# Attention into a maxout FFN on one core: a new hand-written order for batches 0 and 1, and new counts of FFN units per gap

## The chip, the core and the metric

One core of a Trainium2 chip. The time is device microseconds (us) of one execution; three runs of the kernel before gave 296.02, 296.65 and 298.34, median 296.65. The engines are TensorE (PE; its weight loads are PEld), VectorE (DVE), ScalarE (ACT), GpSimd (POOL) and SyncE (SP), which only issues DMA transfers. GpSimd issues some transfers as well, those that turn float32 into bfloat16 on the way.

## What is computed

```python
scores = scale * np.matmul(q, k_all.transpose(0, 1, 3, 2))   # 8 batches, 8 heads, 576 queries, 16+576 keys, D 64
scores = np.where(causal, -1000000000.0, scores)             # the 16 beacon keys are never masked
a = np.exp(scores - scores.max(-1, keepdims=True))
a /= a.sum(-1, keepdims=True) + 1e-09
x = np.matmul(a, v_all)                                      # regrouped to 4608 tokens x 512
h = np.maximum(np.maximum(x @ w1, x @ w2), x @ w3)           # 512 x 768 each
out = h @ w_out                                              # 768 x 512
```

## The kernel before, in words

Heads are taken in pairs: 4 pairs to a batch, 32 in all; two pairs make a quad (0 to 15), and quads 2b and 2b+1 are batch b. For a pair, q and k are brought into transposed form (qT, kT, four buffers each). Pairs 0 to 15 are transposed on TensorE ("half" and "whole" steps, L438, L387, and L396 later), pairs 16 to 31 by DMA: cast to bfloat16, stored to DRAM and fetched with a transposing transfer (`store_pair`, `fetch_pair`, L370, L377). Beacon keys are copied into kT apart ("keys", L458).

The scores of a pair come in four groups (pair, group), each a few matmuls into one PSUM tile (L512), followed by one exponential on ScalarE (L527) that writes `at_sb`. Where a group holds the diagonal it is masked in place: either by GpSimd with an affine select (L546) or by VectorE, which multiplies with a triangle (L544). The values of a quad are taken in two halves of the queries, (quad, 0) and (quad, 1): `emit_pv` (L587) first sums with a column of ones, then multiplies with v; ScalarE inverts the sums (logarithm L607, exponential L609), VectorE multiplies into `xT` (L619), where the tokens of four batches have room.

The FFN is cut into 198 units, 22 for each of 9 blocks of 512 tokens: 18 of x times a weight (L649; the first block in halves, L668), each ending in a copy or a maximum into `hT` on VectorE (L657, L659, L676, L678), and 4 of `hT` times w_out (L685) that are copied to y (L697) and stored. A unit may run as soon as its tokens are in xT; it needs a PSUM bank.

PSUM: a ring of score tiles (two `sc`, and from `widen` on a third, `wide`), two `pv` banks, and at first two `ffn` banks. Scores, transposes, second halves of values and pairs of FFN units ("double") take ring tiles in turn; first halves and single units take the pv banks. Who wants a bank waits for its last reader.

The order of every engine's work is the order in which the program is written (a manual schedule): each engine takes its own instructions strictly in turn. There are two parts.

- Batches 0 and 1 are a list, `first_steps`, run from top to bottom. A step names what is issued, for instance `("mask", 5, 0, "dve")`. `busy n` and the last number of `scores` are spare matmuls on constant data (L476) that keep TensorE occupied, `idle n` such matmuls with half the rows (L417), and the last two numbers of `half` idle transposes ahead of k and of q. `ffn bank kind` is one FFN unit. Loads in the list go to SP, or to GpSimd's own queue (`load w`, `load quad`, `load quad half`, `load w_out`). A gate is a one-element memset by VectorE or GpSimd into the target of a load (L198, L286): the load then waits until that engine has come so far.
- From quad 4 on a loop runs, in which a quad issues: three groups of scores of its first pair, both halves of the values of the quad before, masks, inversion and products; then bursts of further scores with "gaps" between them, each filled with FFN units. `gaps[quad]` has six numbers: the first two stand between the values and the first burst (three groups of scores), the third behind it, the fourth ahead of the second burst (two groups), the last two behind it. A unit whose tokens aren't ready is left out, and so is a double whose two units don't belong together. If the count of units done is odd, one is put ahead of the quad. What is left runs alone at the end.

Casts of the float32 loads run on GpSimd (pairs L248, v L301, first v tiles L313), some on ScalarE. Staging buffers (`st`, eight of them) bound how far SP loads ahead.

## Time and profile before

| | |
|---|---|
| median of three runs | 296.65 us |
| the profiled execution | 297.69 us |
| its span, first to last instruction | 295.80 us |
| mean granted TensorE clock | 0.998 |
| TensorE busy | 281.4 us (95%) |
| VectorE, ScalarE, GpSimd busy | 176.9, 147.5, 116.0 us |
| moved by DMA | 49.51 MB, 167 GB/s over the span |
| TensorE reaches the scores of pair 8 (quad 4) | 60.9 us |

A line of the chain gives start, length and what it was; the chain runs back from the last instruction to what released it each time. A line of a timeline gives start, length, engine, line of the kernel, operation, output<-inputs and count; in brackets is the idle time ahead of it and what ended it. Busy shares of TensorE hold spare matmuls too.

### The profile page before, as it was taken

Reading aid. Unit: us, or ns where it says so; the run is one execution under the profiler, and the core shown is the slowest. Engines: PE = TensorE matmul, PEld = TensorE weight load, DVE = VectorE, ACT = ScalarE, POOL = GpSimd, SP = SyncE. Lnnn points to the kernel's source line nnn. Section 1 sums busy time; section 2 is a strip of 40 time slices with the busy share of each in tenths; the row PEclk is TensorE's granted clock in tenths of the full one; section 3 lists DMA queues with packets and bytes.
Section 4 is the critical chain, followed back from the end, with each engine's and each line's share of the span. In section 5 each row is a group of like instructions: output and inputs, shape, how many; then the busy total and the mean of one; then the engine's idle time right before and its main releaser. Section 6 shows DMA issues by size and latency. Waiting matters only on the chain.

```text
span 295.8 us, 8837 instructions
## 1 busy us (share of the span) xinstructions
PE 281.4 (95%) x3673; PEld 159.1 (54%) x3699; DVE 176.9 (60%) x321; ACT 147.5 (50%) x232; POOL 116.0 (39%) x236
## 2 busy tenths in 40 slices
PE   6899897899999999999999999999999999999995
PEld 3556675664644545454546777545454545444442
DVE  1764678866576566546664656465746564474273
ACT  2665475863834687566735573545555551300300
POOL 3647227253644584436444572357425220000000
PEclk9999999999999999999999999999999999999999
DMA  6999999999986898879898999999658002101103
GB/s 129 157 180 192 201 224 231 192 203 241 248 225 179 201 264 217 190 173 248 224 221 136 232 209 216 211 161 216 189 123 224 2 0 109 38 0 71 71 3 143
DMA packets 95096, 49.51 MB, mean 167 GB/s; under 512 B 64976, under 2 KB 89808, under 8 KB 95056
## 3 DMA queue, kind: packets, MB, share of 16 engines
q1 hardware_dynamic: 89408, 43.73, 63.1%
q0 software_dynamic: 5648, 5.21, 11.5%
q8 instruction: 29, 0.48, 0.8%
q14 instruction: 11, 0.09, 0.1%
HBM read 35.13 MB, written 14.22 MB: 167 GB/s over the span
## 4 chain that ended last, share of the span: by engine, by line
PE 82%; DMA 5%; DVE 5%; ACT 4%; issue 2%; POOL 1%; SPq 0%; ACTq 0%; POOLq 0%
PE pv L649 22%; PE sc L649 12%; PE wide L649 8%; PE sc L685 6%; PE pv L685 6%; PE sc L512 6%; PE sc L587 4%; PE pv L587 4%; DMA whole<-in_k_dram 4%; PE wide L685 3%; PE wide L587 3%; PE wide L512 2%; DVE at_sb L544 2%; ACT at_sb L527 2%; DMA bk<-in_beacon_k_dram 1%
## 5 line engine op out<-in xcount | busy, mean ns | idle before, releaser
L527 ACT ACTIVATE at_sb<-sc 128x736 bf16<-128x736 f32 (+5 forms) x93 | 77.7, 864 | 57.1 <-PE sc L512 56.9
L649 PEld LDWEIGHTS <-w_sb 128*128 128x128 bf16 x648 | 60.7, 98 | 60.6 <-issue 6.1
L546 POOL TENSOR_SCALAR_AFFINE_SELECT at_sb<-at_sb 128x256 bf16<-128x256 bf16 (+3 forms) x138 | 50.4, 383 | 106.4 <-ACT at_sb L527 105.5
L649 PE MATMUL pv<-xT,w_sb 128*128 128x512 bf16 (+1 forms) x337 | 70.8, 349 | 0.4
L527 ACT ACTIVATE at_sb<-wide 128x736 bf16<-128x736 f32 (+3 forms) x35 | 29.9, 855 | 26.0 <-PE wide L512 26.0
L659 DVE TENSOR_TENSOR hT<-hT,pv 128x512 bf16<-128x512 bf16 x50 | 33.8, 685 | 12.9 <-PE pv L649 12.8
L649 PE MATMUL sc<-xT,w_sb 128*128 128x512 bf16 (+1 forms) x183 | 40.4, 361 | 0.6 <-issue 0.2
L248 POOL CAST p<-st 96x768 bf16<-96x768 f32 x40 | 31.9, 821 | 10.7 <-DMA q_dram<-p 10.6
L685 PEld LDWEIGHTS <-hT 128*128 128x128 bf16 x210 | 19.9, 98 | 23.6 <-DVE hT L659 1.0
L619 DVE TENSOR_TENSOR xT<-pv,recip 128x288 bf16<-128x288 f32 (+2 forms) x48 | 14.2, 349 | 28.6 <-ACT recip L609 28.6
L512 PE MATMUL sc<-qT,kT 64*128 64x288 bf16 (+6 forms) x292 | 28.4, 277 | 3.1 <-ACT qT L451 2.5
L512 PEld LDWEIGHTS <-kT 64*128 64x128 bf16 x400 | 14.8, 94 | 25.1 <-issue 17.1
L659 DVE TENSOR_TENSOR hT<-hT,sc 128x1024 bf16<-128x1024 bf16 (+1 forms) x17 | 18.4, 1090 | 13.7 <-PE sc L649 13.7
L587 PEld LDWEIGHTS <-v_sb 128*32 128x32 bf16 (+1 forms) x1408 | 24.6, 96 | 2.3 <-issue 1.0
L649 PE MATMUL wide<-xT,w_sb 128*128 128x512 bf16 (+1 forms) x111 | 24.5, 364 | 0.1
L657 DVE CAST hT<-pv 128x512 bf16<-128x512 f32 x24 | 16.2, 687 | 7.2 <-PE pv L649 7.2
L685 PE MATMUL sc<-w_out_sb,hT 128*128 128x512 bf16 x79 | 19.1, 380 | 0.3
L301 POOL CAST v_sb<-st 128x1536 bf16<-128x1536 f32 (+2 forms) x21 | 18.4, 893 | 2.1 <-issue 2.1
L685 PE MATMUL pv<-w_out_sb,hT 128*128 128x512 bf16 x81 | 18.9, 379 | 0.3 <-issue 0.2
L668 PEld LDWEIGHTS <-w_sb 128*128 128x128 bf16 x144 | 13.3, 98 | 3.9 <-issue 1.4
L609 ACT ACTIVATE recip<-lnd 128x288 f32<-128x288 f32 x32 | 14.2, 443 | 1.0
L697 DVE COPY y<-pv 128x512 f32<-128x512 f32 x14 | 9.7, 691 | 8.1 <-PE pv L685 7.5
(112 smaller groups left out, 286.2 us busy)
## 6 DMA issues: line engine op xcount, KB each, us to landing
st<-in_q_dram SPq DMA_DIRECT2D x48, 144.0 KB, 3.8
st<-in_k_dram SPq DMA_DIRECT2D x48, 144.0 KB, 3.9
st<-in_v_dram SPq DMA_DIRECT2D x24, 256.0 KB, 5.2
out_dram<-y SPq DMA_DIRECT2D x9, 512.0 KB, 3.4
out_dram<-y SPq DMA_DIRECT2D x17, 256.0 KB, 2.8
w_sb<-in_moe_w_dram POOLq DMA_DIRECT2D x6, 384.0 KB, 7.4
q_dram<-p SPq DMA_DIRECT2D x16, 144.0 KB, 2.8
k_dram<-p SPq DMA_DIRECT2D x16, 144.0 KB, 2.4
```

Of the source, the lines that this page charges most:

```text
L248: cast(t16.rearrange("p r h d -> p h r d"), st[0:QP, i * NQ2 : (i + 1) * NQ2].rearrange("p (h r d) -> p h r d", h=2, r=QR),)
L301: cast(v_sb[0:n, t:t1].rearrange("p t h d -> p (t h d)"), st[0:n, (t - t_lo) * H * D : (t1 - t_lo) * H * D],)
L512: nc.tensor.matmul(ps[:, e, off : off + q1 - q0], kT[hs, 128 * t : 128 * t + 128], qT[hs, q0:q1], start=True, stop=True, tile_position=(64 ...
L527: nc.scalar.activation(out=both_heads(p, gi), in_=ps[:, :, 0 : g_width(p, gi)], func=AF.Exp, scale=scale)
L546: nc.gpsimd.affine_select(out=view, in_=view, compare_op=ALU.is_ge, fill=0.0, base=x0, pattern=[[0, 2], [1, hi - lo]], channel_multiplier=-1,)
L587: nc.tensor.matmul(ps[bank][32 * j : 32 * j + 32, lo + q0 - qa : lo + qb - qa], lhsT, at_view(PPQ * quad + j // 2, t, j % 2, q0, qb), star ...
L609: nc.scalar.activation(out=recip, in_=lnd, func=AF.Exp, scale=-1.0)
L619: nc.vector.tensor_mul(xT[:, 2 * g + part - 1, c0 + ca : c0 + cb], ps[bank][:, lo : lo + cb - ca], recip[:, ca:cb],)
L649: nc.tensor.matmul(dst[:, o0 : o0 + n], w_in[i][:, ct, 128 * (ft + f) : 128 * (ft + f + 1)], xT[:, ct, x0 : x0 + n], start=(ct == 0), stop ...
L657: (by_act if alone[0] else by_dve)(h, ps)
L659: nc.vector.tensor_max(h, h, ps)
L685: nc.tensor.matmul(ps[:, t - tt] if two else ps, hT[:, ft, 128 * t : 128 * (t + 1)], w_out_sb[:, ft, :], start=(ft == 0), stop=(ft == n_ft ...
```

## The change

It touches the list and the counts, and the helpers that the list needs. In the list:

- Start: GpSimd makes the triangle first and then issues its two quad loads; SP loads q of pair 1, k and q of pair 0, k of pair 1, then the beacon keys; before it was k of pair 1, q and k of pair 0, keys, q of pair 1. The first v load is gated by GpSimd instead of VectorE. 27 spare matmuls stand ahead of the first transposes (19 before, with 4 `idle` ones, which go), and 42 more idle transposes, in three turns.
- 16 of the 32 masks were on VectorE, 14 are now: (1,0), (1,2), (1,3), (2,2), (3,3), (5,3), (6,1), (6,2), (6,3) go to GpSimd and (1,1), (2,1), (3,1), (3,2), (4,0), (4,1), (5,1) come from it.
- The loads of w2, of the second whole quad of batch 1, of v of batch 1 and of pair 9 come later in the list, those of w_out and the cast of pair 9 earlier; several get gates. Four copies of transposed q and k change between ScalarE and VectorE.
- The list has 17 FFN units as before, in other places.

By quad, 4 to 15, the counts of units that really run are (up to the next quad's start, with the odd ones): before 11, 14, 10, 12, 9, 13, 10, 11, 12, 10, 11, 14; after 12, 12, 13, 10, 8, 16, 12, 10, 14, 8, 6, 14.

```diff
--- before.py
+++ after.py
     def L(fn, *a):
-        return lambda: fn(*a)
+        return lambda *more: fn(*a, *more)
...
-    def load_v(b, piece):
+    def load_v(b, piece, gate=None):
         for t in range(*V_PIECES[piece]):
-            load_v_tile(b, t, v_stage(b, t))
+            dst = v_stage(b, t)
+            if gate and t == V_PIECES[piece][0]:
+                gate.memset(dst[32:33, 0, 0:1], 0.0)
...
-    def next_load(n=1):
+    def next_load(n=1, gate=None):
         for _ in range(n):
             if loads:
-                loads.pop(0)()
+                loads.pop(0)(*([idle[gate]] if gate else []))
...
     first_steps = [
+        ("triangle",),
+        ("load quad half", 1, 0),
+        ("busy", 17),
+        ("load half", 1, 0, "sp"),
+        ("load half", 0, 1, "sp"),
+        ("load half", 0, 0, "sp"),
+        ("identity",),
+        ("cast half", 1, 0, "dve"),
         ("load half", 1, 1, "sp"),
-        ("load half", 0, 0, "sp"),
-        ("load half", 0, 1, "sp"),
         ("load keys 0", "sp"),
-        ("load quad half", 1, 0),
-        ("busy", 15),
+        ("load v0", 0, "pool"),
         ("cast half", 0, 1, "dve"),
-        ("idle", 2),
-        ("load half", 1, 0, "sp"),
-        ("cast half", 1, 1, "dve"),
-        ("triangle",),
-        ("load v0", 0, "dve"),
-        ("busy", 4),
+        ("busy", 10),
         ("cast keys 0", "act"),
-        ("identity",),
         ("cast half", 0, 0, "act"),
-        ("half", 0, 0, "ffn", "act", 0, 0),
+        ("half", 0, 0, "ffn", "act", 0, 7),
+        ("load v0", 1, "pool"),
+        ("cast half", 1, 1, "act"),
         ("turn keys 0",),
+        ("half", 1, 0, "ffn", "dve", 2, 5),
         ("keys", 2, "pool"),
+        ("keys", 3, "act"),
+        ("keys", 1, "act"),
+        ("load quad half", 0, 1),
+        ("scores", 0, 0, 3),
+        ("half", 3, 0, "ffn", "dve", 0, 0),
+        ("load w", 0),
+        ("mask", 0, 0, "dve"),
         ("cast v0", 0),
-        ("scores", 0, 0, 1),
-        ("keys", 3, "act"),
-        ("keys", 1, "dve"),
-        ("load v0", 1),
-        ("cast half", 1, 0, "dve"),
-        ("half", 1, 0, "pv", "dve", 0, 0),
-        ("half", 3, 0, "ffn", "dve", 0),
         ("scores", 1, 0, 4),
-        ("half", 2, 0, "pv", "dve", 6),
-        ("load quad half", 0, 1),
+        ("half", 2, 0, "pv", "dve", 6, 0),
+        ("mask", 1, 0, "pool"),
+        ("cast v0", 1),
+        ("load v0", 2),
         ("scores", 3, 0, 3),
-        ("mask", 1, 0, "dve"),
-        ("scores", 2, 0, 5),
-        ("mask", 0, 0, "dve"),
-        ("load v0", 2),
-        ("cast v0", 1),
+        ("scores", 2, 0, 4),
         ("cast v0", 2),
-        ("load w", 0),
-        ("values", 0, 0, "pv"),
+        ("values", 0, 0, "pv", 0, 4, 0),
+        ("half", 0, 1, "ffn", "act", 0, 7),
+        ("load quad half", 1, 1),
         ("invert",),
+        ("scores", 0, 2, 7),
+        ("mask", 3, 0, "dve"),
         ("mask", 2, 0, "dve"),
-        ("load quad half", 1, 1),
-        ("half", 0, 1, "ffn", "dve", 0, 0),
-        ("mask", 3, 0, "dve"),
-        ("scores", 0, 2, 7),
+        ("scores", 0, 3, 0),
         ("multiply",),
+        ("values", 1, 0, "ffn", 0, 4, 0),
+        ("invert",),
+        ("mask", 0, 3, "pool"),
+        ("half", 1, 1, "pv", "act", 0, 0),
         ("load keys 1",),
-        ("values", 1, 0, "ffn"),
-        ("invert",),
-        ("scores", 0, 3),
-        ("half", 1, 1, "pv", "dve", 0, 0),
-        ("mask", 0, 3, "pool"),
         ("load v0", 3, "dve"),
+        ("multiply",),
+        ("scores", 0, 1, 0),
         ("load v0", 4, "pool"),
-        ("multiply",),
-        ("scores", 0, 1, 2),
-        ("scores", 1, 2, 3),
+        ("scores", 1, 2, 2),
+        ("ffn", "ffn", 0),
         ("ffn", "ffn", 0),
         ("mask", 0, 1, "pool"),
-        ("scores", 1, 3),
-        ("mask", 1, 3, "dve"),
+        ("load w", 1),
+        ("scores", 1, 3, 0),
+        ("half", 2, 1, "pv", "dve", 0, 0),
+        ("scores", 1, 1, 0),
         ("ffn", "ffn", 0),
-        ("load w", 1),
-        ("ffn", "ffn", 0),
-        ("scores", 1, 1, 0),
+        ("cast v0", 3),
+        ("half", 3, 1, "pv", "dve", 0, 0),
         ("load quad", 1, 0),
         ("mask", 0, 2, "pool"),
+        ("scores", 2, 3, 0),
+        ("mask", 1, 1, "dve"),
+        ("mask", 1, 3, "pool"),
+        ("mask", 1, 2, "pool"),
+        ("cast v0", 4),
+        ("load v", 1, 0, "dve"),
+        ("scores", 2, 2, 7),
+        ("cast keys 1", "pool"),
+        ("scores", 3, 2, 3),
+        ("values", 0, 1, "pv", 0, 4, 0),
+        ("scores", 3, 3, 0),
+        ("invert",),
+        ("ffn", "ffn", 0),
+        ("multiply",),
+        ("mask", 2, 3, "pool"),
+        ("turn keys 1",),
         ("load w", 2),
-        ("mask", 1, 1, "pool"),
-        ("cast v0", 3),
-        ("cast v0", 4),
-        ("half", 2, 1, "pv", "dve", 0),
-        ("scores", 2, 2, 6),
-        ("mask", 1, 2, "dve"),
-        ("half", 3, 1, "ffn", "dve", 0),
-        ("load quad", 1, 1),
-        ("mask", 2, 2, "dve"),
-        ("scores", 2, 3, 0),
-        ("scores", 3, 2, 2),
-        ("values", 0, 1, "pv", 0, 4, 0),
-        ("invert",),
         ("scores", 2, 1),
...
+        ("scores", 5, 3, 0),
+        ("load quad", 1, 1),
+        ("mask", 4, 0, "dve"),
+        ("load v", 1, 1, "pool"),
+        ("keys", 7, "pool"),
+        ("mask", 4, 2, "dve"),
         ("mask", 5, 0, "dve"),
-        ("scores", 5, 1),
-        ("mask", 4, 0, "pool"),
-        ("scores", 5, 2),
...
-        ("whole", 6, "ring", "act"),
+        ("whole", 6, "ring", "dve"),
+        ("mask", 5, 2, "dve"),
+        ("mask", 5, 1, "dve"),
+        ("ffn", "ring", 0),
+        ("keys", 6, "act"),
         ("cast v", 1, 0),
-        ("mask", 5, 2, "dve"),
-        ("mask", 5, 1, "pool"),
+        ("ffn", "pv", 1),
+        ("scores", 6, 2, 0),
+        ("scores", 6, 0, 0),
         ("cast pair", 8),
-        ("mask", 4, 3, "pool"),
-        ("ffn", "ring", 0),
-        ("ffn", "pv", 0),
-        ("scores", 6, 2),
+        ("ffn", "pv", 1),
+        ("load w_out",),
+        ("scores", 6, 1, 0),
+        ("values", 2, 0, "ring", 0, 4, 0),
+        ("load", 1, "pool"),
+        ("cast pair", 9),
+        ("invert",),
         ("keys", 9, "pool"),
-        ("scores", 6, 0, 0),
-        ("load", 2),
-        ("scores", 6, 1, 0),
-        ("cast v", 1, 1),
-        ("mask", 5, 3, "dve"),
-        ("ffn", "pv", 0),
-        ("values", 2, 0, "ring", 0, 4, 0),
-        ("invert",),
-        ("keys", 8, "act"),
-        ("mask", 6, 0, "dve"),
-        ("mask", 6, 1, "dve"),
         ("whole", 7, "ring"),
         ("ffn", "pv", 1),
         ("multiply",),
+        ("load", 2, "dve"),
         ("scores", 6, 3, 0),
-        ("mask", 6, 2, "dve"),
+        ("cast v", 1, 1),
+        ("mask", 6, 2, "pool"),
+        ("mask", 6, 1, "pool"),
+        ("mask", 6, 3, "pool"),
         ("scores", 7, 2, 0),
+        ("load", 1, "dve"),
+        ("load", 1, "dve"),
+        ("keys", 8, "pool"),
         ("whole", 8, "pv", "dve"),
         ("scores", 7, 1, 0),
-        ("mask", 6, 3, "dve"),
-        ("load", 1),
-        ("load", 1),
-        ("scores", 7, 0),
-        ("load", 1),
-        ("values", 2, 1, "ring"),
+        ("scores", 7, 0, 0),
+        ("mask", 6, 0, "dve"),
+        ("values", 2, 1, "ring", 0, 4, 0),
         ("invert",),
+        ("scores", 7, 3, 0),
+        ("mask", 7, 2, "pool"),
+        ("whole", 9, "ring", "act"),
         ("multiply",),
-        ("scores", 7, 3, 1),
-        ("load w_out",),
-        ("ffn", "pv", 1),
+        ("mask", 7, 3),
         ("mask", 7, 1, "pool"),
-        ("cast pair", 9),
-        ("mask", 7, 3),
-        ("whole", 9, "ring", "dve"),
+        ("load", 1, "pool"),
+        ("ffn", "pv", 0),
         ("mask", 7, 0, "pool"),
...
     gaps = {
-        4: (2, 2, 2, 1, 1, 2),
-        5: (4, 2, 1, 1, 4, 2),
-        6: (2, 2, 1, 2, 1, 2),
-        7: (2, 2, 1, 7, 1, 1),
-        8: (3, 1, 2, 2, 0, 1),
-        9: (3, 1, 0, 1, 2, 5),
-        10: (5, 0, 1, 2, 0, 2),
-        11: (3, 0, 0, 3, 4, 3),
-        12: (4, 2, 2, 0, 1, 2),
-        13: (2, 2, 3, 6, 1, 1),
-        14: (3, 0, 1, 2, 2, 2),
-        15: (2, 2, 1, 4, 3, 2),
+        4: (3, 2, 2, 2, 1, 1),
+        5: (4, 2, 3, 2, 2, 0),
+        6: (2, 2, 2, 2, 2, 2),
+        7: (1, 1, 1, 7, 1, 1),
+        8: (1, 0, 2, 1, 3, 1),
+        9: (4, 2, 1, 5, 2, 6),
+        10: (5, 0, 2, 2, 1, 2),
+        11: (5, 1, 1, 2, 0, 3),
+        12: (7, 1, 2, 2, 0, 2),
+        13: (3, 1, 3, 14, 2, 3),
+        14: (2, 0, 2, 0, 0, 2),
+        15: (7, 0, 4, 4, 1, 1),
     }
```

## The prediction

> **What bounds the kernel now.** I read the page first (busy shares, slices, chain), then busy time by stage, then the chain of waits and the timelines of the first 62 us, last single quads.
>
> ```profile
> PE 281.4 (95%) x3673; PEld 159.1 (54%) x3699; DVE 176.9 (60%) x321; ACT 147.5 (50%) x232; POOL 116.0 (39%) x236
> DMA  6999999999986898879898999999658002101103
> PE 82%; DMA 5%; DVE 5%; ACT 4%; issue 2%; POOL 1%; SPq 0%; ACTq 0%; POOLq 0%
> ```
> ```profile
> 8.00:34.00 26.00, 24.01 (x437) 15.69 (x431) 17.02 (x49) 16.92 (x28) 15.80 (x31) 1.00 1.12 185
> 34.00:60.00 26.00, 22.39 (x442) 17.20 (x443) 20.82 (x39) 17.05 (x27) 9.18 (x17) 1.00 1.12 213
> 60.00:126.00 66.00, 64.98 (x854) 34.51 (x859) 42.47 (x71) 39.27 (x65) 34.35 (x68) 1.00 0.89 219
> 126.00:189.00 63.00, 62.37 (x938) 38.80 (x946) 36.25 (x62) 35.33 (x55) 30.21 (x61) 1.00 0.92 211
> ```
>
> The second fence has, by stage: its ends and length, busy us (and instructions) of PE, PEld, DVE, ACT, POOL, then the granted clock, the DMA share and GB/s. TensorE carries 82% of the chain. From 60 us on it idles 1 us in 66; from 8 to 60 us it idles 5.6 us, and part of its busy time there is idle work (34 spare matmuls in scores, 19 ahead). So an order can win a few us before 60 and can mostly only lose after. The granted clock is 1.00 from 8 us on: nothing to gain there. The DMA engines run at 9 tenths until 200 us.
>
> ```profile
> 2.25 4.44 DMA bk<-in_beacon_k_dram
> 12.12 1.93 DVE at_sb L544 x6
> 22.96 11.02 DMA whole<-in_k_dram
> 34.02 0.45 PE fps L387 x12
> 43.91 3.64 DVE at_sb L544 x2
> 48.85 0.65 ACT qT L451
> ```
> ```profile
> 29.88 2.64 PE L668 MATMUL fps<-xT,w_sb 128*128 128x256 bf16 x22 [0.34 <-DMA w_sb<-in_moe_w_dram]
> 34.02 0.45 PE L387 MATMUL fps<-ident,whole 96*64 96x96 bf16 x12 [0.80 <-DMA whole<-in_k_dram]
> 49.54 0.58 PE L512 MATMUL sc<-qT,kT 64*128 64x464 bf16 x6 [2.21 <-ACT qT L451]
> ```
>
> The first fence is the chain (start, length, what): six links that are not TensorE's own work. The second shows TensorE's idle time in brackets. The 2.21 us come from the DVE link: two masks on VectorE take 3.64 us (one mask: median 275, longest 2303 ns in the view of at_sb) while GpSimd works without a break:
>
> ```profile
> 43.91 3.64 DVE L544 TENSOR_TENSOR at_sb<-at_sb,tri 128x224 bf16<-128x224 bf16 x2
> 43.73 1.46 POOL L301 CAST v_sb<-st 128x1536 bf16<-128x1536 f32 x1 [2.13 <-issue]
> 45.47 1.59 POOL L248 CAST p<-st 96x768 bf16<-96x768 f32 x2
> ```
>
> Behind them in VectorE's order stand an FFN maximum (0.67), kT of pair 6 (0.74), then ScalarE's qT (0.65), and only then scores (6,2).
>
> **The change, part by part.** The sum is made on the profiled execution: 297.69 us (span 295.80 and 1.89 around it), 1.04 over the median 296.65; I apply it to the median.
>
> 1. *Start, to the first FFN unit (20.3 us).* GpSimd makes the triangle (0.22 + 0.29) before its two quad loads (issue 0.81 + 0.67), so the SP loads meet them later. The beacon keys go from fourth to fifth on SP (0.50 later), and ScalarE casts k of pair 1 (0.51) ahead of the key copies. The first exponential, at 9.31 now, can come 1.3 later (0.50 + 0.51 + copies 0.33) or 0.6 earlier; nearest to the middle, I take 0. The value tiles' gate moves from VectorE (memset at 6.88) to GpSimd behind the identity, near 4.2, so three v loads go 2.7 us earlier. Mask (1,0) on GpSimd costs 0.32 to 0.41 an instruction against 0.28, and two v casts (0.61 each) stand behind it, awaited by values (0,0): I place their end near 14.9 (now 15.1). ScalarE takes q of pair 0 and pair 1 from VectorE, which lets the multiply of quad 1 end 0.6 sooner. First FFN unit: -0.4 (ends -0.9, +1.5).
> 2. *21 to 36 us.* The loads of GpSimd's queue land one behind the other, some 2 us apart: whole k of quad (1,0) landed 11.02 after its issue, at 33.98. In the new order cast v0 3 (waits for its load, 25.4 now, 0.6 earlier by its gate) stands ahead of this load, so it is issued at about 25 instead of 22.3. It still has only the two pieces of w1 ahead; w2 goes behind the keys' cast, and the second whole load behind mask (3,3). By the present spacing it lands at 33.5, with v of batch 1 issued later perhaps at 31. TensorE reaches these transposes at 32.4 (work 1.1 less between). I take -0.8 (ends -1.6, and +4 should the landing keep 13 to 15 us, as whole of quad (1,1) took). w2 and w_out are needed over 6 and 3 us after they land; if that cover is gone each costs its lateness.
> 3. *44 to 54 us.* Mask (5,0) moves ahead of cast v(1,0), and so pays 0.28 twice instead of 3.64. Masks (5,2), (5,1) come behind q and k of pair 6, both now on VectorE (0.75 + 0.75, ScalarE's 0.65 gone), and still meet cast pair 8. Nearest row 2.30 for such a mask, best 0.28: I take 1.8 for the two. Waiting behind them on VectorE: three FFN results, the first in the ring tile that scores (6,1) need, 0.85 late. Of the idle 2.21 this leaves 0.85, and 0.2 goes with qT: -1.2 (ends -2.2, +3.4).
> 4. *54 us to the values of quad 3.* In the present order cast pair 9 (two of 0.82) stands between the masks of pair 7, and the stretch from values (2,1) idles 0.51 + 0.30, then about 1 us before the values of quad 3. In the new order pair 9 is cast before whole 7 and four masks end GpSimd's list. The gate memset of pair 14 on VectorE waits for cast v(1,1), and whole 8's copies stand behind it: 0.4 late. -0.9 (ends -1.6, +1).
> 5. *Idle work.* 8 spare matmuls more (0.135 warm), 42 idle transposes more (half of 0.04 each), 4 idle matmuls gone: 1.7 us of TensorE. All but the seven pairs in turn (0,1), 0.28, lie in waits for the first casts; counted in 1. Uncovered: +1.7.
> 6. *Gaps.* FFN units are only moved, so time is lost only where a gap gets too short. Quads 7 and 8 had 4 units behind the second values, the first two in a free ring tile; now 2 and 1, single, in banks that the multiply still reads (in quad 7 values end at 113.65, the multiply of half 0 at 114.44): +0.7 each. Quad 14 has two instead of three. Quad 11 shows what three small ones cost:
>
> ```profile
> 174.66 0.89 DVE L619 TENSOR_TENSOR xT<-wide,recip 128x288 bf16<-128x288 f32 x3 [0.72 <-ACT recip L609]
> 175.46 1.21 DVE L659 TENSOR_TENSOR hT<-hT,sc 128x1024 bf16<-128x1024 bf16 x1
> 176.73 0.34 PE L512 MATMUL sc<-qT,kT 64*128 64x288 bf16 x4 [0.28 <-DVE hT L659]
> ```
>
>    The double's tile is free 3.5 us after the values' end (173.20), and the third scores need it. With 1.73 of units and 0.4 of scores TensorE waits 1.3: +1.3 for quad 14; quads 11 and 9, now fuller, give back 0.5 and 0.7. Sum +1.5 (ends 0, +3).
>
> *DMA.* Costed at 0: attention of quads 10 to 13 gets later by the units moved ahead. Pair 24's transposes were issued at 178.3 and used at 186.5, landing in 3 to 4.3: some 3 us of cover; gone, up to +2.2.
>
> Sum: -0.4 - 0.8 - 1.2 - 0.9 + 1.5 = -1.8, so 296.65 - 1.8 = 294.85, say 294.8.
>
> *A rule beside this.* In the row one mask stood 2.30 us, across two casts, a mask and a copy of GpSimd. The Trainium skill, "SBUF — State Buffer", section "SBUF: two separate sides", says VectorE with two SBUF inputs and GpSimd take a shared port pair for a whole instruction, the loser waiting fully. The trace agrees that it waits, not that one instruction is its length. By that rule each mask of step 3 waits for one cast (0.82) at most, and it is 0.3 better: 294.5. It speaks against step 1 too: masks put on GpSimd hold the pair 0.1 longer each.
>
> **Rivals.**
> - *All of the early gain stays.* The gaps cost nothing since ScalarE runs ahead of the rows I used, and the masks of step 3 meet no cast: 294.8 - 1.5 - 0.85 = 292.4. For it: TensorE idles only 1 us in 66 past 60. Against: quad 11's wait.
> - *No change.* Early time is given back to the DMA engines (9 tenths): the pairs' loads end when they did, 2 us return: 296.8. For it: the DMA row. Against: 8 us and more of cover until quad 9.
> - *Slower: VectorE stands through GpSimd's whole run.* In the new order cast v(1,0) 1.46, pair 8 1.59, w_out's issue 0.85, pair 9 1.59, v(1,1) 1.21 and three masks 1.2 follow each other, 7.9 us, if pair 9's load has landed. Masks (5,2), (5,1), started 1.8 in, would stand 6.1 instead of 1.8, with TensorE behind them: 294.8 + 4.9 (with its own late copies) = 299.7. It decides from a stand of 6 us on. For it: a mask stood across four instructions. Against: pair 9 is loaded so late that GpSimd should pause before its cast.
>
> **How the numbers follow.** About 1% (3 us) is what a measurement of this kernel can tell from no change. Forecast 0.46 (within 1.5 of 294.8), of which 0.10 lies under 293.7; all of the gain 0.20; no change 0.14; slower 0.20, of which 0.19 is over 299.6. Faster 0.30, same 0.51, slower 0.19. The range takes in the two outer cases but for their far halves: 291.8 to 299.5.
>
> **What would show it.** Right: scores (6,2) without the 2.21, quad 4's first scores 2 to 3 us earlier than 60.9, 0.7 to 1.3 of idle time at the first scores behind the values of quads 7, 8, 14. Wrong: whole of quad (1,0) landing past 33.5, a mask on VectorE over 2.3 us behind 44 us, or DMA named as releaser after 150 us.

## The result, and the profile after

The changed kernel takes 297.52 us (median of 20 runs, 296.75 to 299.72); before, beside it on the same chip, 295.98 (293.92 to 301.15). The ratio is 1.0064, 95% interval 1.0036 to 1.0092: 1.9 us slower, with 1.1 to 2.7 in the interval. (Ratios leave out executions that took over 1.5% more than the fastest of their kernel; medians hold all, and by them the difference is 1.5.) The forecast was 1.8 faster. The profiled executions are 298.05 (span 296.3) and 297.69 (span 295.8), so the profile of before is one of its longer executions, and a comparison of these two shows only 0.5 of the difference.

The page after, then busy time by stage (columns as in the prediction):

```profile
PE 284.5 (96%) x3722; PEld 160.6 (54%) x3745; DVE 169.4 (57%) x310; ACT 149.5 (50%) x236; POOL 118.1 (40%) x247
DMA  8699998999998899799989998996492002101203
PE 85%; ACT 5%; DVE 3%; DMA 2%; issue 2%; POOL 2%; SPq 1%; ACTq 0%; POOLq 0%
```
```profile
8.00:34.00 26.00, 23.34 (x453) 15.22 (x448) 12.56 (x38) 17.82 (x32) 14.64 (x34) 1.00 0.96 156
34.00:60.00 26.00, 25.21 (x475) 19.04 (x475) 19.81 (x48) 18.68 (x30) 12.44 (x28) 1.00 1.05 209
60.00:126.00 66.00, 64.22 (x843) 34.09 (x848) 41.11 (x69) 39.37 (x65) 33.87 (x66) 1.00 0.98 226
126.00:189.00 63.00, 62.17 (x850) 37.62 (x852) 36.37 (x60) 33.35 (x51) 29.36 (x58) 1.00 0.97 222
```

TensorE idles 0.8 us from 34 to 60 where it idled 3.6, but 2.7 instead of 2.0 from 8 to 34, and 1.8 instead of 1.0 from 60 to 126. Part of its busy time before 34 is idle work. The chain of waits at the start is where the time went:

```profile
2.75 6.19 DMA bk<-in_beacon_k_dram
8.96 0.62 ACT bk L867
9.57 0.42 ACT h L220
10.40 0.40 ACT qT L451
10.80 0.41 ACT h L220
11.54 0.20 POOL kT L463
12.01 1.33 POOL quad L229 x2
13.90 0.56 POOL w_sb L326
14.46 0.62 POOL v_sb L316
15.07 0.90 POOL at_sb L551 x3
15.97 1.12 POOL v_sb L316 x2
17.13 0.66 PE pv L592 x24
```

Start, length, what: the beacon keys land at 8.94 us (before: 6.69). ScalarE casts them, then q of pair 0, then k of pair 1 (the step `cast half 1 1`, below also k of pair (1,1)). GpSimd copies the keys, and only then comes to two quad issues, two weight issues, a cast, the mask that was VectorE's, and two casts. Before, the chain went from the keys to the first scores and VectorE's masks. The three places that the forecast named in the middle did improve. The masks on VectorE behind 44 us now take 1.27 for five instructions, and GpSimd's long cast of v begins as the fifth does:

```profile
45.93 1.27 DVE L549 TENSOR_TENSOR at_sb<-at_sb,tri 128x224 bf16<-128x224 bf16 x5
46.93 1.59 POOL L304 CAST v_sb<-st 128x1536 bf16<-128x1536 f32 x1
48.47 1.65 POOL L248 CAST p<-st 96x768 bf16<-96x768 f32 x2
```

The wait of 2.21 us of TensorE for qT at 49.5 is gone (the scores' line has no idle time in brackets), and the 0.80 ahead of the whole transposes is 0.1:

```profile
49.29 0.58 PE L517 MATMUL sc<-qT,kT 64*128 64x464 bf16 x6
L392 PE MATMUL fps<-ident,whole 96*64 96x96 bf16 x24 | 0.9, 209 | 0.1
```

Below, positions read from the profiles, in us: when the keys landed, the first values, the first FFN unit (by its first weight load), the start of quad 4 (by the FFN unit put ahead of it; its first scores come 1.0 later, at 59.87 in the changed kernel), the end. The last two columns are the length of the two stretches behind the first FFN unit, which hold the same FFN units and the same attention in every row.

| kernel | keys | values | FFN | quad 4 | end | FFN to quad 4 | quad 4 to end |
|---|---|---|---|---|---|---|---|
| before | 6.69 | 13.46 | 20.32 | 59.88 | 295.80 | 39.56 | 235.92 |
| before, again | 6.23 | 13.46 | 20.06 | 58.92 | 295.26 | 38.86 | 236.34 |
| changed | 8.94 | 16.16 | 23.11 | 58.80 | 296.34 | 35.69 | 237.54 |
| e1 v behind keys | 7.86 | 15.09 | 22.02 | 58.53 | 296.45 | 36.51 | 237.92 |
| e2 old counts | 7.66 | 14.89 | 21.82 | 57.75 | 295.02 | 35.93 | 237.27 |
| e3 old list, new counts | 6.10 | 13.33 | 19.93 | 56.83 | 294.11 | 36.90 | 237.28 |
| h1 old start, old counts | 6.32 | 13.56 | 20.02 | 58.12 | 293.60 | 38.10 | 235.48 |
| e5 keys fourth | 6.23 | 14.57 | 21.51 | 57.49 | 295.37 | 35.98 | 237.88 |
| e8 start undone | 5.96 | 13.39 | 20.24 | 55.62 | 293.25 | 35.38 | 237.63 |
| e12 same, warm, old counts | 5.91 | 13.35 | 20.20 | 56.01 | 293.50 | 35.81 | 237.49 |
| e13 before, warm | 7.15 | 14.25 | 20.91 | 58.78 | 295.21 | 37.87 | 236.43 |

The changed kernel loses 2.8 us to the first FFN unit, wins 3.9 to quad 4 and loses 1.6 behind it. Before's own middle varies by 2.7 us between executions (36.90 to 39.56 in four profiles of its list); against their mean of 38.3 the win is 2.6, and the whole some 1.5 slower, near what the times say.

One wait in the last two columns has no releaser in the profile ("issue"). These are lines of before, of the changed kernel and of e2 (the new list with the counts of before), and one of e2's DMA queues from 59 to 60 us:

```profile
57.73 0.37 PE L587 MATMUL sc<-at_sb,v_sb 128*32 128x96 bf16 x17 [0.51 <-issue]
62.16 0.34 PE L592 MATMUL pv<-at_sb,v_sb 128*32 128x192 bf16 x13 [0.67 <-issue]
62.01 0.34 PE L592 MATMUL pv<-at_sb,v_sb 128*32 128x192 bf16 x13 [1.56 <-issue]
q8 instruction: 1, 0.02, 8.0%
```

TensorE stands in the middle of values, and the profile names nothing that it waits for. Counted through all traces, there are 24 such waits of over 0.25 us ahead of 80 us. They come behind 1217, 1729, 1985 or 2497 instructions of TensorE, give or take one, so multiples of 256 apart; and each ends 1.3 to 1.75 us after a transfer of 16 KB of the queue that the page calls "instruction" (in e2 it ran from 59.22 to 60.50). So I read them as waits for TensorE's next instructions; no run tests that. In the table such waits lie mostly ahead of quad 4 in before (0.51), its copy (0.95) and h1 (1.25), and mostly behind its start in the other rows (0.3 to 1.8 there; none in e3). Taken out, the last column is 235.5 to 236.1 with the counts of before on either list, 236.8 to 236.9 with the new counts on the new list, and 237.3 on the old one (e3).

### The profile page after: what moved, and what is told of

It reads as the page before. It is cut to its first block, busy times and chain, and to the rows that moved or that the text cites. A ratio compares the mean times of both kernels' runs of the same rounds, so it can differ in the third digit from the quotient of the medians.

```text
span 296.3 us, 8943 instructions
## 1 busy us (share of the span) xinstructions
PE 284.5 (96%) x3722; PEld 160.6 (54%) x3745; DVE 169.4 (57%) x310; ACT 149.5 (50%) x236; POOL 118.1 (40%) x247
## 4 chain that ended last, share of the span: by engine, by line
PE 85%; ACT 5%; DVE 3%; DMA 2%; issue 2%; POOL 2%; SPq 1%; ACTq 0%; POOLq 0%
PE pv L654 18%; PE sc L654 16%; PE wide L654 8%; PE pv L690 8%; PE sc L690 6%; PE sc L517 6%; PE sc L592 4%; PE pv L592 4%; PE wide L517 2%; ACT at_sb L532 2%; DMA bk<-in_beacon_k_dram 2%; PE fps L673 2%; PE pv L673 2%; PE wide L592 2%; PE wide L690 1%
## 5 line engine op out<-in xcount | busy, mean ns | idle before, releaser
L532 ACT ACTIVATE at_sb<-sc 128x992 bf16<-128x992 f32 (+5 forms) x90 | 75.5, 863 | 66.8 <-PE sc L517 66.8
L654 PEld LDWEIGHTS <-w_sb 128*128 128x128 bf16 x648 | 60.9, 98 | 60.8 <-issue 5.1
L654 PE MATMUL pv<-xT,w_sb 128*128 128x512 bf16 (+1 forms) x269 | 57.5, 354 | 0.8 <-DVE xT L624 0.6
L654 PE MATMUL sc<-xT,w_sb 128*128 128x512 bf16 (+1 forms) x237 | 51.7, 358 | 0.6
L532 ACT ACTIVATE at_sb<-wide 128x928 bf16<-128x928 f32 (+3 forms) x38 | 32.7, 859 | 15.2 <-PE wide L517 15.2
L664 DVE TENSOR_TENSOR hT<-hT,sc 128x1024 bf16<-128x1024 bf16 (+1 forms) x20 | 23.3, 1166 | 17.0 <-PE sc L654 16.4
L664 DVE TENSOR_TENSOR hT<-hT,pv 128x512 bf16<-128x512 bf16 x40 | 26.9, 685 | 8.6 <-PE pv L654 8.5
L654 PE MATMUL wide<-xT,w_sb 128*128 128x512 bf16 (+1 forms) x125 | 26.5, 352 | 0.2
L690 PE MATMUL pv<-w_out_sb,hT 128*128 128x512 bf16 x104 | 25.0, 380 | 0.8 <-DVE xT L624 0.6
L702 DVE COPY y<-pv 128x512 f32<-128x512 f32 x18 | 12.4, 691 | 12.4 <-PE pv L690 11.5
L662 DVE CAST hT<-pv 128x512 bf16<-128x512 f32 x20 | 13.7, 690 | 6.9 <-PE pv L654 6.9
```

Source lines behind the costliest of these rows:

```text
L532: nc.scalar.activation(out=both_heads(p, gi), in_=ps[:, :, 0 : g_width(p, gi)], func=AF.Exp, scale=scale)
L654: nc.tensor.matmul(dst[:, o0 : o0 + n], w_in[i][:, ct, 128 * (ft + f) : 128 * (ft + f + 1)], xT[:, ct, x0 : x0 + n], start=(ct == 0), stop ...
L664: nc.vector.tensor_max(h, h, ps)
L690: nc.tensor.matmul(ps[:, t - tt] if two else ps, hT[:, ft, 128 * t : 128 * (t + 1)], w_out_sb[:, ft, :], start=(ft == 0), stop=(ft == n_ft ...
```

## The experiments

Times are medians of 12 executions (6 for e6 and e7), ratios against the kernel before, run beside them. The positions are in the table above. Two profiles of one kernel differ by a microsecond and more at a given place, and the intervals are some 0.35% wide on either side, so most verdicts rest on places in the profile.

**First: which part loses?** A copy of before for the spread; the changed kernel with the first v load gated by a copy out of the keys' tile, so that it is issued when the keys have landed; the changed list with the FFN counts of before; the list of before with the new counts.

> The kernel before once more, unchanged: a second profile of it beside new times, to see how far single executions differ. Both theories: the same time as before within the interval. If the profile before had a piece of bad luck in it (its execution took 297.69 against a median of 295.98), this span comes out 1 to 2 us under 295.8 and the place shows; if not, within 0.5.

> The new order with one edit: the gate of the first v load is a copy out of the beacon keys on VectorE, so that v tiles 0 and later start only when the keys have landed. Theory (early v loads hold up the keys, which landed at 8.93 instead of 6.68, and ScalarE's casts behind them): keys near 6.8, first scores 2.0 to 2.5 us earlier than 11.5, first FFN unit 1.5 to 2.5 earlier than 23.1, and 1.5 to 2.5 us off the time of the new order, that is 0 to 0.3% under before. Rival 1 (the keys are late because they stand fifth on SP beside two quad loads): keys stay past 8.3, time within 0.5 of the new order, 0.4 to 0.8% over before. Rival 2 (the DMA engines set the pace of the first 60 us): keys early, but quad 4 starts within 0.5 of 58.8 and the time stays.

> The new order of batches 0 and 1 with the counts of units per gap of before. Theory (the new counts cost 1.3 us by waits behind the values of quads 7, 8 and 14): idle time at these three places gone, 1.0 to 1.6 us off the new order, 0.1 to 0.3% over before. Rival (the counts are fitted to the new order, and the old ones cost as much elsewhere): within 0.5 us of the new order.

> The order of before with the new counts of units per gap: the other half of the change alone. Theory: 1.0 to 1.6 us slower than before (0.35 to 0.55%), waits of 0.7 behind the values of quads 7 and 8 and 0.9 at the burst of quad 14. Rival (the new counts cost nothing, all of the loss is at the start): within 0.2% of before.

```diff
# e1_v_after_keys, against the changed kernel
-        if gate:
+        if gate == "keys":
+            nc.vector.tensor_copy(dst[32:33, 0, 0:1], bk32_0[0:1, 0, 0:1])
+        elif gate:
             idle[gate].memset(dst[32:33, 0, 0:1], 0.0)
...
-        ("load v0", 0, "pool"),
         ("cast half", 0, 1, "dve"),
+        ("load v0", 0, "keys"),
```

Measured: the copy 297.27, 1.0011 (0.9972 to 1.0049); e1 297.47, 1.0032 (1.0000 to 1.0065); e2 296.71, 0.9998 (0.9966 to 1.0030); e3 296.53, 1.0001 (0.9960 to 1.0042). In e1 the keys landed at 7.86 us, in e2, with v loaded early as in the changed kernel, at 7.66: the early v loads are not what holds the keys. The start's loss is in both, the new counts alone do not make it. By the profiles the counts cost 1.0 from quad 4 to the end on the old list (e3 237.28 against 236.2, the mean of the three profiles of the old list with the old counts), and 0.4 on the new one (237.7, the mean of the changed kernel, e1, e5 and e8, against 237.4, that of e2, e12 and e14). The 0.4 is too small, since the instruction wait is longer in e2, e12 and e14 (1.5 to 1.8) than in the four others (0.7 to 1.1): without it the counts cost 1.1 on the new list, and some 1.3 on the old. The waits that they bring are the same in e3 as in the changed kernel (0.61 behind the values of quads 7 and 8, 0.33 in quad 14), and e2 has none of them. The time of e2 is below that of the changed kernel (0.9998 against 1.0064, the intervals just apart); that of e3 can't be told from before's.

**Second: the keys' place, GpSimd's queue, the old start.** e5 moves one load; e6 one load of GpSimd; h1 takes the old list up to the second inversion, then the new one, with the old counts; e7 has the moves of e5 and e6 and the old counts.

> The changed kernel with one move: the beacon keys are loaded fourth on SP instead of fifth, ahead of k of pair (1,1). In the changed kernel's profile, and in two variants with the same start, the keys landed at 8.93, 7.86 and 7.66 us against 6.1 to 6.7 in the list of before, the first values began 7.2 us after that landing, and the first FFN unit 14.2 us after it. Theory (the keys' landing sets the start): they land at 6.2 to 6.9, first scores at 8.8 to 9.5, first values at 13.4 to 14.1, first FFN unit at 20.4 to 21.1; time 1.3 us under the changed kernel's, ratio to before 1.002. Rival (the DMA engines are shared by six loads at once, whatever their order): the keys land at 7.5 or later and nothing moves, ratio 1.006. Second rival (the first weights bound the first FFN unit by themselves): keys and values move, the first FFN unit stays at 21.8 or later.

> The changed kernel with one move: the load of the second quad half (two issues on GpSimd, 1.33 us together) goes behind the third cast of v instead of ahead of the first. Theory (the keys' landing alone): the way from that landing to the first values stays 7.2 us, first FFN unit 14.2 us after the landing, ratio to before 1.006. Rival (GpSimd's queue behind the landing is the bound: key copies, 1.33 of quad issues, 1.6 of weight issues, casts of v, a mask): that way shrinks to 5.9 us and the first FFN unit comes 12.9 us after the landing, ratio 1.002.

> The list of before up to the second inversion (all of the start), the changed kernel's list from there on, the FFN counts of before in the gaps. Theory (the new start loses 2 to 3 us, the new order from the first FFN unit to quad 4 wins 2.5 to 3): keys land near 6.2, first FFN unit at 20.0 to 20.4, the way from whole 6 to scores (6,2) takes 2.5 us, quad 4 begins at 56 to 57 (before: 58.9 and 59.9), time 2.3 us under before, ratio 0.992. Rival (the middle gains only because everything before it is late, and loads end it at a given moment): quad 4 begins at 57.8 or later, ratio 0.997 or more.

> The changed kernel with both moves (keys fourth on SP, second quad half behind the third cast of v) and the FFN counts of before in the gaps. If landing and GpSimd's queue add up: first values at 12.2 to 13, first FFN unit at 19 to 20, quad 4 at 55.5 to 56.5, ratio to before 0.990. If the keys' landing alone counts: first FFN unit at 20.4 to 21.1, quad 4 at 56.5 to 57.3, ratio 0.994. If the first weights bound it: first FFN unit at 21.8 or later, quad 4 near 57.8, ratio 0.998.

```diff
# e5_keys_fourth
-        ("load half", 1, 1, "sp"),
         ("load keys 0", "sp"),
+        ("load half", 1, 1, "sp"),
# e6_quad_later
-        ("load quad half", 0, 1),
...
         ("cast v0", 2),
+        ("load quad half", 0, 1),
```

e5: 295.98, 0.9996 (0.9965 to 1.0028). The keys land at 6.23 as the theory said, the first FFN unit comes at 21.51, 1.6 earlier than in the changed kernel and 0.3 to 0.5 earlier than in e2 and e1: less than the landing won. The chain has the reason:

```profile
1.34 4.73 PE pv L481 x17
6.11 2.10 PE pv L481 x10
8.21 0.42 PE fps L411 x14
8.63 0.15 PE fps L443 x6
8.80 0.40 ACT qT L451
9.20 0.41 ACT h L220
```

The 27 busy matmuls and 14 idle transposes now end last, 8.63, and the cast of k of pair (1,1) stands in ScalarE's queue ahead of the key copies. So three things lay one behind the other, and the keys had hidden two. Yet this one move takes the loss out of the time: the interval of e5 ends at 1.0028, that of the changed kernel begins at 1.0036. e6: 302.69, 1.0225 (1.0175 to 1.0276), e7: 300.03, 1.0131 (1.0085 to 1.0177). In e6 the first values still came 7.2 us after the keys' landing (8.02), as in the changed kernel, e1 and e2: the two quad issues in GpSimd's queue are not what holds their start, the keys are. Further on the two runs tell nothing of that queue, since the moved load is late itself:

```profile
16.08 0.63 POOL quad L229
16.71 4.27 DMA quad<-in_k_dram
21.02 0.45 PE fps L443 x6
```

The turn of half (2,0) waits for it until 21.02, and the first FFN unit comes at 27.36; in e7, for the same reason, at 25.43, so what it was to tell apart stays untold. h1: 296.85, 1.0033 (0.9996 to 1.0070). The start is the old one, and the middle takes 38.1 instead of 35.7: the rival's number. But no load ends it: 1.25 of the difference is the instruction wait, which fell ahead of quad 4 here, and 1.10 is a wait of TensorE for qT at 47.24. That one comes from VectorE's masks, which stand again. The line of all five, the fifth alone, and the cast; below them the fifth and the cast in the changed kernel:

```profile
42.72 2.53 DVE L549 TENSOR_TENSOR at_sb<-at_sb,tri 128x224 bf16<-128x224 bf16 x5
43.71 1.55 DVE L549 TENSOR_TENSOR at_sb<-at_sb,tri 128x256 bf16<-128x256 bf16 x1
43.65 1.46 POOL L304 CAST v_sb<-st 128x1536 bf16<-128x1536 f32 x1
46.92 0.28 DVE L549 TENSOR_TENSOR at_sb<-at_sb,tri 128x256 bf16<-128x256 bf16 x1
46.93 1.59 POOL L304 CAST v_sb<-st 128x1536 bf16<-128x1536 f32 x1
```

The order in the list is the same. What differs is who begins first: in the changed kernel the fifth mask is 0.01 us ahead of the cast and takes 0.28; in h1 it is 0.06 behind and stands until the cast has ended. From quad 4 on h1 is the fastest row, 235.48, so the new order as a whole is not refuted by it.

**Third: the start undone, and three sets of counts.** e8: four edits, the keys fourth, 8 busy matmuls fewer, the idle transposes of two turns gone (14 steps of two, so 28), k of pair (1,1) cast behind the key copies, the turn of half (1,0) behind the first scores. e9, e10 and e11 are e8 with other counts.

> The changed kernel with four things of its start undone together: the keys fourth on SP; 8 busy matmuls and the 14 idle transposes of two turns fewer; ScalarE casts k of pair (1,1) behind the key copies; the turn of half (1,0) stands behind the first scores. Keys fourth alone brought the first scores only from 10.25 to 11.5 down to 9.92 us, because the idle matmuls ran to 8.21, the idle transposes to 8.63, and the cast of k of pair (1,1) (0.41) stood ahead of the key copies. Theory (these bound the start one behind the other): first scores at 8.2 to 9.0, first values at 13.2 to 14.0, first FFN unit at 20.0 to 20.8. Rival (the landing of the first weights, at 21.0 to 22.8 in the changed list, bounds the first FFN unit whatever the scores do): first FFN unit at 21.3 or later. The way from quad 5 to the end of the gaps stays 175.6 us. Ratio to before 1.000 by the theory, 1.004 by the rival.

> The kernel with four things of the start undone, and in the gaps of quads 7 and 8 the units of before ahead of and behind the values (quad 7: 2, 2 instead of 1, 1; quad 8: 3, 1 instead of 1, 0), taken from quad 13 (9 instead of 14): as many units as before. The way from quad 5 to the end of the gaps took 175.55 to 175.59 us with the new counts and, with one unit of 0.94 more, 174.89 to 175.36 with the old ones, so the new ones cost about 1.6. Theory (quads 7 and 8 wait 0.7 each for the multiply): 174.1 to 174.3. Rival (the loss is in quads 9 to 14): 175.5 or more. Ratio to before 1.4 us under that of the kernel with four things undone.

> The kernel with four things of the start undone, and the counts of before in quad 14 alone (10 units instead of 6), four of them taken from quad 13: as many units as before. Theory (quad 14 loses 1.3 behind its second values): the way from quad 5 to the end of the gaps takes 174.3 instead of 175.6 us. Rival (quads 7 and 8 hold all of the loss, or the long gap of quad 13 covered it): 175.5 or more.

> The kernel with four things of the start undone and all FFN counts of before. If the start is mended and the middle keeps its 35.7 to 36.3 us from the first FFN unit to quad 4: first FFN unit at 20.4, quad 4 at 56.4, the way from quad 5 to the end of the gaps 174.9, ratio to before 0.992. Rival (an early start brings the middle back to 38 us, as with the start of before: 38.1): quad 4 at 58 or later, ratio 0.998 or more.

```diff
# e8_start_four, with the keys fourth as in e5
-        ("busy", 17),
+        ("busy", 15),
...
-        ("busy", 10),
+        ("busy", 4),
         ("cast keys 0", "act"),
         ("cast half", 0, 0, "act"),
-        ("half", 0, 0, "ffn", "act", 0, 7),
+        ("half", 0, 0, "ffn", "act", 0, 0),
         ("load v0", 1, "pool"),
-        ("cast half", 1, 1, "act"),
         ("turn keys 0",),
-        ("half", 1, 0, "ffn", "dve", 2, 5),
+        ("cast half", 1, 1, "act"),
...
         ("scores", 0, 0, 3),
+        ("half", 1, 0, "ffn", "dve", 0, 0),
# e9_quads_7_8, against e8
-        7: (1, 1, 1, 7, 1, 1),
-        8: (1, 0, 2, 1, 3, 1),
+        7: (2, 2, 1, 7, 1, 1),
+        8: (3, 1, 2, 1, 3, 1),
...
-        13: (3, 1, 3, 14, 2, 3),
+        13: (3, 1, 3, 9, 2, 3),
# e10_quad_14, against e8
-        13: (3, 1, 3, 14, 2, 3),
-        14: (2, 0, 2, 0, 0, 2),
+        13: (3, 1, 3, 10, 2, 3),
+        14: (3, 0, 1, 2, 2, 2),
```

e8: first values 13.39, first FFN unit 20.24: the start's loss of 2.8 us is these four edits, and the rival with the first weights is out. Quad 4 begins at 55.62, so here the middle keeps its gain from an early start too. Yet the time is 297.27, ratio 1.0052 (1.0009 to 1.0095): the profiled execution is the shortest of its twelve. e11 (old counts) 295.70, 1.0021 (0.9979 to 1.0062), its first values at 16.16. Why, stands in its busy time by stage (its profile is its longest execution), and below it the same of e8:

```profile
4.00:8.00 4.00, 2.34 (x26) 1.34 (x25) 0.12 (x2) 1.24 (x3) 0.08 (x2) 0.98 1.30 208
8.00:12.00 4.00, 3.68 (x40) 2.12 (x37) 2.25 (x6) 2.04 (x7) 3.18 (x6) 0.50 1.32 184
12.00:16.00 4.00, 4.00 (x49) 2.21 (x49) 1.46 (x5) 1.73 (x2) 1.95 (x6) 0.66 1.09 154
```
```profile
4.00:8.00 4.00, 2.65 (x29) 1.55 (x27) 0.81 (x2) 1.61 (x6) 0.00 (x0) 1.00 1.39 227
8.00:12.00 4.00, 3.53 (x69) 2.26 (x67) 2.96 (x10) 2.56 (x6) 3.26 (x6) 1.00 1.36 185
12.00:16.00 4.00, 3.95 (x92) 2.48 (x91) 0.51 (x2) 2.57 (x5) 3.38 (x7) 1.00 1.03 154
```

The clock is the third number from the right: half speed from 8 to 12 us in e11, full in e8, with the same list. With 15 and 4 busy matmuls TensorE stood 1.60 us (e11) and 1.29 (e8) ahead of the first turn. Of the 48 executions of e8 to e11, 14 had a mean granted clock under 0.9935. A mean of 0.994 is one stretch of 3.41 us at half speed, as the clock record of e10 has one (63.45 to 66.86), so this bound counts, for the most part, executions with two or more.

e9 (295.92, 1.0027, 0.9990 to 1.0064): quads 7 and 8 did get their time back, and quads 13 and 14 took it. TensorE's idle time is 0.83 less from 60 to 189 us (0.68 and 0.34 against 1.03 and 0.82), and 1.25 more from 189 to 250. These are the rows from 189 to 250 of e8, then of e9, and two waits of e9 that e8 does not have:

```profile
189.00:250.00 61.00, 60.09 (x766) 30.02 (x767) 36.35 (x62) 30.73 (x48) 23.25 (x49) 1.00 0.52 124
```
```profile
189.00:250.00 61.00, 58.84 (x755) 29.71 (x760) 34.93 (x58) 29.78 (x47) 23.30 (x49) 1.00 0.45 115
215.62 0.39 PE L517 MATMUL wide<-qT,kT 64*128 64x288 bf16 x4 [0.74 <-ACT at_sb L532]
222.24 0.34 PE L517 MATMUL wide<-qT,kT 64*128 64x288 bf16 x4 [0.70 <-DVE hT L662]
```

From quad 5 to the end of the gaps it took 175.75 us against 175.57, where 174.2 was expected. But the edit does not do what its expectation says. By the rules of the loop, a double whose two units don't belong together is left out, and the 14 of quad 13 asks for doubles alone: it runs no unit in e8. With 9 it runs one, which in e8 ran behind the second burst. So quad 13 has 8 units in both; the three that quad 8 has more come from quad 9, the two of quad 7 from its own long gap. What lost is, by these two lines, the one unit that moved ahead of the burst: the next scores follow the burst at once and wait for ScalarE (0.74), and quad 14's wait 0.70 for VectorE. e10 (296.62, 1.0036, 0.9997 to 1.0075) took 175.91. There too quad 13 gives nothing: the four units come from quad 15 (12 instead of 14) and from the two that ran ahead of the last values. The 1.3 for quad 14 did not come back. Its profile has a clock of 0.97 from 60 to 120 us and is its longest execution.

**Fourth: idle work and the clock, and the counts once more.** e12 is e11 with 17 and 6 busy matmuls, e13 is before with 17 and 8 instead of 15 and 4, e14 is e5 with the old counts.

> The kernel with four things of the start undone and the FFN counts of before, with 17 and 6 busy matmuls at the start instead of 15 and 4, so that TensorE has idle work until about 7.2 us, when the first turn can begin. With 15 and 4 it stood 1.29 to 1.60 us before that turn, and one profile shows the granted clock at 0.50 from 8 to 12 us and the first values at 16.16 instead of 13.3 us; 14 of the 48 executions of the four kernels with 15 and 4 had a mean granted clock under 0.9935, none of 56 of the lists with 17 and 10. Theory (the idle work keeps the clock): no execution of 12 under 0.9935, first values at 13.3 to 13.9, first FFN unit at 20.1 to 20.8, median 294.2, ratio to before 0.994. Rival (chance, or another cause): 3 or 4 of 12 under 0.9935, median 295.7, ratio 1.000.

> The kernel before with 17 and 8 busy matmuls at the start instead of 15 and 4, nothing else. 15 of 92 of its executions, and 4 of 12 in another set, had a mean granted clock under 0.9935, and its median is 296.0 to 296.9 against 295.5 to 295.9 of those at the full clock. Theory (the idle work keeps the clock in the start): no execution of 12 under 0.9935, median 295.9, ratio 0.998. Rival (idle work changes nothing): 2 or 3 of 12 under it, ratio 1.000; or it lies on the path of the first turn (7.2 to 7.8 us): first scores later than 8.4 us, ratio 1.002.

> The changed kernel with the keys fourth on SP (its idle work kept) and the FFN counts of before. The same with the new counts had a median of 295.98, with all 12 executions at a full granted clock. Theory (the new counts cost 1.6 between quad 5 and the end of the gaps): that way takes 174.9 instead of 175.56 with one unit of 0.94 more in it, median 294.5, ratio 0.995. Rival (the counts cost nothing in the time): median 296.0, ratio 1.000.

```diff
# e12_warm_start_gaps, against e11; e13 has the same places in the list of before, with 17 and 8
-        ("busy", 15),
+        ("busy", 17),
...
-        ("busy", 4),
+        ("busy", 6),
```

e12: 296.02, 0.9995 (0.9962 to 1.0029); no execution under 0.9935, TensorE stands 0.39 ahead of the first turn, first values 13.35, first FFN unit 20.20. It is 1.5 under the changed kernel and cannot be told from before; the 1.8 us that its profile is ahead of the copy of before did not show in the medians (0.4). e13: 296.91, 1.0052 (1.0020 to 1.0084); none under 0.9935 either, but slower all the same. In its profile the keys landed at 7.15 and the first turn came at 8.25, behind them and not behind the idle work. Whether the keys land late because of it can't be said from one profile. e14: 295.82, 1.0013 (0.9974 to 1.0052), against 0.9996 with the new counts: the counts' cost does not show in the time. From quad 4 to the end it took 237.34 against 237.88, or 235.9 against 236.9 without the instruction wait. Its middle took 37.94, with the clock at half speed from 22.19 to 25.60.

## Why the prediction was wrong

**The failed step is the first, the start: "First FFN unit: -0.4 (ends -0.9, +1.5)".** It measured +2.8, beyond even its outer end, and it is larger than the whole of the -1.8. Three pieces of it failed.

- *The keys "go from fourth to fifth on SP (0.50 later)".* The issue is 0.50 later. But in fourth place they landed 3.59 to 4.90 us after it, in fifth 4.92 to 6.19: at 5.84 to 7.15 us by the one, at 7.66 to 8.94 by the other. The step priced the issue and not the flight. e5, which moves the keys alone, shows that the place decides; e8, which undoes the rest too, brings the first FFN unit back to 20.24.
- *"The first exponential ... can come 1.3 later or 0.6 earlier; nearest to the middle, I take 0."* There was no row for the middle. The 0.51 of ScalarE's cast lay on the path (0.41 in the chain), as did the turn of half (1,0) ahead of the first scores, which the step did not list: from the keys' landing to the first scores it took 3.1 us instead of 2.2.
- *"I place their end near 14.9": the casts of v.* They ended at 17.09, and the values, begun at 16.16, waited for them (17.13 in the chain). The early gate of the v loads, from which the step took its gain, won nothing: v waited for GpSimd, GpSimd for the key copies and its issues behind them.

**Step 2, whole k, -0.8: right in size.** The way from the first FFN unit to the second half of quad 1's values went from 14.08 (13.45 to 14.01 in three other profiles of that list) to 12.91. Whole k took 8.26 us to land instead of 11.02 and was awaited no longer (0.1). It landed at 35.40, past the 33.5 that the forecast named as a sign of being wrong, but that did no harm, since TensorE came to these transposes 2.3 later too (35.11).

**Step 3, masks beside casts, -1.2: right, but not safe.** The way from the first transpose of whole 6 to the first matmul of scores (6,2) is 2.49 us in the changed kernel, e1, e2, e5 and e8, against 4.76 before; other executions of that list had 3.69, 3.44 and 3.65. So the profile of before showed a long one, and against those the gain is 1.0 to 1.2, what the step took. The two masks that it priced at 1.8, (5,2) and (5,1), took 0.38 and 0.85, each until the cast that had begun ahead of it ended; that bears out the rule beside the sum. h1 had 3.65.

**Step 4, up to quad 3's values, -0.9: in part a wait that only moved.** From scores (6,2) to quad 4: 9.51 against 10.34 (10.78, 9.63 and 9.63 in others). The 0.51 of idle time that the step counted as a gain is the instruction wait. It is 0.95 in the copy and missing in the two at 9.63, so against those the order itself gained 0.1. And it is not won: in the new list it comes behind the start of quad 4, at the values of quad 3, 0.67 us in the changed kernel and 1.56 in e2. The new list takes 1.1 us more from quad 4 to the end with the same old counts (237.4, the mean of e2, e12 and e14, against 236.2); without this wait nothing of that is left.

**Step 5, idle work at 0: wrong in both directions.** Where the keys came on time, it lay on the path of the first turn (8.63 in e5 instead of 7.06 in e8). And it goes with a steadier clock: with 19 busy matmuls, 44 of 205 executions were under 0.9935 (14 of 48 in e8 to e11, 23 of 121 of before, 7 of 36 in its copy, e3 and h1); with 27, 2 of 68 (changed, e1, e2, e5, e14), and with 23 and 25 none of 24 (e12, e13). In e6 and e7, which have 27 too but stand for the late load, it was 8 of 12. That idle work is the cause is argued: one stretch at half speed (0.994) is as frequent with 27 (13 of 68) as with 19 (29 of 205), and two of the three profiles of lists with early keys that show one have it far from the start (e10 at 63.45, e14 at 22.19). The step had its price and left out this possible use.

**Step 6, the gaps, +1.5 (ends 0, +3): right in its mechanism.** From quad 4 to the end the changed kernel loses 1.6 against before. The instruction wait is 0.67 of it; without it the counts cost 1.1 on the new list. The waits stand where the step put them, behind the values of quads 7 and 8 (0.7 each forecast), and in quad 14 (1.3 forecast, 0.33 measured):

```profile
115.47 0.39 PE L654 MATMUL pv<-xT,w_sb 128*128 128x512 bf16 x1 [0.61 <-DVE xT L624]
129.99 0.39 PE L690 MATMUL pv<-w_out_sb,hT 128*128 128x512 bf16 x1 [0.62 <-DVE xT L624]
224.17 0.30 PE L517 MATMUL wide<-qT,kT 64*128 64x288 bf16 x2 [0.33 <-issue]
```

All six profiles with the new counts as they are have the first two, none of those with the old counts; the wait of 0.28 in quad 11 went, part of what the step gave back.

Steps 2 to 6 came to -1.4 by the forecast, and from the first FFN unit to the end the changed kernel is 2.25 faster than the profile of before, 1.8 than the mean of its three profiles in the table (275.0). The sum failed in the first twenty microseconds. The slower rival (masks standing through GpSimd's whole run, behind 44 us) was not what happened: its two masks took 1.2 together, and its 6.1 did not come. That the kernel came out slower all the same has another cause, the start. Of the other signs that the forecast named, quad 4's first scores came 1.0 us earlier than 60.9 (59.87) and not 2 to 3, since the start took the rest, and behind 150 us no DMA is the releaser of a wait over 0.25.

What stays open: the medians of e8, e12 and e14 do not show all that their profiles won. Intervals of 0.35% hold 1 us, and one execution of a list differs from the next by more, in part by the instruction waits and the half-speed stretches. Among executions with a mean clock of 0.997 or more alone, the medians are 297.3 (changed), 296.0 (e5), 295.9 (e8), 295.7 (e12), 295.5 (e14) and 294.1 (e11), and 295.4 to 295.8 for before; picked by their outcome, they show a direction at most. Why the load of 16 KB comes too late in some executions and not in others is open too.

## What to carry to other kernels

Price a load that is moved back in a queue by its landing, not by its issue, and follow every engine that waits for it to the work queued behind that wait: here one late small tile moved the whole start. A chain of hidden bounds shows one at a time, so undo all of them together once, then apart. Before counting an idle stall of one profiled execution as a gain, look whether other executions have it, and whether the stall belongs to the place or to the count of instructions ahead of it.

## What the runs showed of the hardware

- A load of 32 KB that was issued 0.50 us later, behind one more load of 144 KB, took 4.92 to 6.19 us to land in four profiles (changed, e1, e2, e6), and 3.59 to 4.90 as the fourth in the others.
- The granted clock fell to 0.50 after a stand of TensorE of 1.60 us behind 4.5 us of work (e11), and after one of 1.70 at 63.45 (e10), and stayed at 1.00 after 1.85 us behind 6.9 us (the changed kernel). The Trainium skill, "TensorE: Matmul & The Clock Gate", section "What's actually happening", puts the fall after an idle window of some 3.4 us; e11 and e10 show a shorter stand to be enough, each in one profile. In e7, where TensorE was busy for 1.36 of the 4 us from 16 to 20, the clock was 0.57 for the next four.
- A mask of VectorE that began 0.01 us ahead of a cast of GpSimd took 0.28 (the changed kernel); the same one that began 0.06 behind it took 1.55, to 0.15 behind the cast's end (h1).
- TensorE stood 0.3 to 1.8 us at multiples of 256 of its instructions, until 1.3 to 1.75 us after a 16 KB transfer of the instruction queue had ended: 24 times ahead of 80 us in 17 profiles, 19 of them among values, where up to 223 instructions begin within 2 us.
